# Two loads moved to ScalarE's DMA queue, and the output projection's products in another order, in a decode step of attention and feed-forward

## The chip, the cores and the metric

The kernel runs on one core of a Trainium2 chip. The metric is the device time of one execution in microseconds (us). Of the kernel before there are three timed runs: 120.58, 120.75 and 120.88, median 120.75.

The engines are TensorE (PE, with its weight loads as PEld), VectorE (DVE), ScalarE (ACT), GpSimd (POOL) and SyncE (SP). SP and ACT issue transfers between the chip's main memory and the on-chip memory, each on a queue of its own; 16 DMA engines carry them out. "SPq" and "ACTq" are the instructions of these two engines that issue. P, below, is the 128 partitions of the on-chip memory.

## The reference

For eight sequences, one token each, of width 512: a layer norm, an attention over the last 1024 positions of a cache (32 query heads, 8 cached heads, 128 wide), a GEGLU feed-forward of the same normalized token, and a product of the two:

```
xn = layernorm(x)                                  # 8 x 512
q = xn @ wq                                        # 8 x 4096: 32 heads of 128
p = softmax(q k^T / sqrt(128))                     # over 1024 positions, 4 query heads per cached head
s = (p v) @ wo                                     # 4096 x 512
g = silu((gelu(xn @ w_gate) * (xn @ w_up)) @ w_down)   # 512 -> 1792 -> 512
out = x + s * g
```

All inputs are bf16. They come to 47.5 MB: 33.6 MB of cache, wq and wo with 4.2 MB each, and the three feed-forward weights with 1.8 MB each.

## The kernel before, in words

**Order.** The kernel is written out under a manual schedule: each engine does its work in the order of the text. All loads but x are issued by SP, in this order: wo's first quarter (L106, a tile of its own, `wo_first`), wq (L109, one DMA of 4 MB), then the cache by sequence b, keys and values in two DMAs of 1 MB each (L84: k0, k1, v0, and in the loop L402 k of b+2 and v of b+1), then w_gate and w_up (L426), w_down (L429) and the rest of wo (L439). The cache tiles and the late weights go round eight slots of 2 MB (`slot`, L67); a load waits until the tile that had the slot is done with. ACT issues the five DMAs of x (L79) at the start and the store of the result (L513) at the end.

**Start.** DVE and ACT normalize x (L145 to L152), PE turns it (L166), and 32 products with wq give q (L260).

**Attention.** For each of the eight sequences DVE turns the keys into `kT` (L248), PE makes the scores (L309), DVE and ACT the softmax (L319 to L340), DVE turns the probabilities (L344), and PE multiplies them with the values (L354). `gather` (L374) and `regroup` (L376 to L398) bring the results of four sequences into `oT`, the left operand of the output projection. Its second call (L443) completes oT.

**Feed-forward.** PE makes `z_ps` and `u_ps` from w_gate and w_up (L453, 16 products each). ACT and DVE do the GELU on z: a square (L463), two DVE steps (L464, L467), a tanh (L469), and three DVE steps (L470, L471, L473) of which the last multiplies by u. DVE turns the result into `hT` (L476). PE makes `f_ps` with w_down (L482, 56 products), and ACT and DVE make the gate `g_sb` of it (L490 to L494).

**Output projection.** `wo` has four quarters u of 1024 rows. In a quarter, partition p holds rows 8p to 8p+7, as j = 0 to 7; "row j" below is that row of all 128 partitions, 128 KB. There are four products for each u and j (t = 0 to 3, a quarter of the columns each), 128 in all. They come behind w_down's products on PE, u = 0 to 3 in order, and add up in `s_ps`:

```
for u in range(NU):
    for j in range(8):
        for t in range(4):
            nc.tensor.matmul(s_ps[32 * t : 32 * t + 32, :], oT[:, j, u, :],
                wo[u][:, j, t * DT : (t + 1) * DT],
                start=(u == 0 and j == 0), stop=(u == NU - 1 and j == 7))
```

The quarter u = 3 is loaded in three pieces, rows 0 to 4, 5 and 6, and 7 (L437), so that PE can begin with the first. Then DVE multiplies `s_ps` by the gate (L509), adds x (L511), and ACT stores.

Of the kernel before, what the change touches and what calls it, by code (L numbers as in the profile page):

```python
# [11 lines left out]
FP32 = mybir.dt.float32  # L12
# [9 lines left out]
def kernel(  # L22
# [13 lines left out]
    nc = tc.nc  # L36

    B, Sq, D = A_x.shape
# [7 lines left out]
    P = nc.NUM_PARTITIONS  # L46
# [7 lines left out]
    DT = D // 4  # L54
# [12 lines left out]
    def slot(name):  # L67
        i = taken[0] % N_SLOTS
        taken[0] += 1
        if i >= 2:  # L70
            return ring.tile([P, 2 * ROW], BF16, name=name, tag="slot")
        if not late:
            late.append(ctx.enter_context(tc.tile_pool(name="late", bufs=2)))
        return late[0].tile([P, 2 * ROW], BF16, name=name, tag="slot")
# [22 lines left out]
    def load_v(b):  # L97
        v_sb[b] = load_cache(A_v_cache, b, "v_sb")

    NU = Hq // 8  # L100
    wo_src = [
        A_wo[u * 1024 : (u + 1) * 1024, :].rearrange("(p j) d -> p j d", j=8)
        for u in range(NU)
    ]
    wo_first = first.tile([P, 8, D], BF16, name="wo_first")
    nc.sync.dma_start(out=wo_first, in_=wo_src[0])  # L106
    wq_v = A_wq.rearrange("(p k) n -> p k n", k=NK)
    wq_all = wq_pool.tile([P, NK, Hq * Dh], BF16, name="wq_sb")
    nc.sync.dma_start(out=wq_all, in_=wq_v)  # L109
# [9 lines left out]
        out=ident,  # L119
        in_=ident,  # L120
# [13 lines left out]
        out=xpad,  # L134
        in_=xpad,
# [17 lines left out]
        out=xhat,  # L153
# [8 lines left out]
    with tc.tile_pool(name="ps_x", bufs=1, space=PSUM) as ps_x:  # L162
# [7 lines left out]
        for t in range(4):  # L170
# [4 lines left out]
                start=True,  # L175
                stop=True,
# [12 lines left out]
        out=hv,  # L189
        in_=hv,  # L190
# [7 lines left out]
        out=neg_st,  # L198
        in_=neg_st,
# [8 lines left out]
        out=neg_mv,  # L208
        in_=neg_mv,
# [11 lines left out]
    for g in range(NG):  # L221
        nc.vector.tensor_reduce(
            out=sel[:, g, g * qd : (g + 1) * qd],
            in_=ident.rearrange("p (t g h) -> p g h t", t=4, g=NG)[:, g],
# [5 lines left out]
        out=own, in_=ident.rearrange("p (i e) -> p e i", e=8), axis=AX.X, op=ALU.add  # L230
    )
    pick = consts.tile([P, 4 * NU], BF16, name="pick")
    with nc.allow_low_precision(reason="sums of zeros and a single one"):
        nc.vector.tensor_reduce(
            out=pick, in_=ident.rearrange("p (a e) -> p a e", e=8), axis=AX.X, op=ALU.add
        )
    oT = keep.tile([P, 8, NU, 32], BF16, name="oT")
# [18 lines left out]
    with tc.tile_pool(name="ps_q", bufs=1, space=PSUM) as ps_q:  # L256
        q_ps = [ps_q.tile([P, 512], FP32, name=f"q_ps{i}") for i in range(8)]
        for k in range(NK):
            for i in range(8):
# [4 lines left out]
                    start=(k == 0),  # L264
                    stop=(k == NK - 1),
                )
        for half in range(2):
            for i in range(4 * half, 4 * half + 4):
                e = nc.vector.tensor_copy if i % 4 == 3 else nc.scalar.copy
# [7 lines left out]
    for j in range(4):  # L277
        sl = slice(32 * j, 32 * j + 32)
        for m in range(2):
            for g in range(NG):  # L280
                e = nc.scalar.copy if (4 * j + 2 * m + g) % 3 == 2 else nc.vector.tensor_copy
# [145 lines left out]
        wgu.append(tv)  # L427
    wd = slot("wd_sb")[:, 0 : NJ * D].rearrange("p (j d) -> p j d", d=D)
    nc.sync.dma_start(out=wd, in_=B_w_down.rearrange("(p j) d -> p j d", j=NJ))  # L429
    wo = [wo_first]  # L430
    for u in range(1, NU):
        if u % 2 == 1:
            pair = slot("wo_sb").rearrange("p (v j d) -> p v j d", v=2, d=D)
        t = pair[:, (u - 1) % 2]
        pieces = [(0, 8)]
        if u == NU - 1:
            pieces = [(0, 5), (5, 7), (7, 8)]  # L437
        for a, z in pieces:
            nc.sync.dma_start(out=t[:, a:z, :], in_=wo_src[u][:, a:z, :])  # L439
        wo.append(t)  # L440

    gather(B - 1)
    regroup(1)  # L443
# [2 lines left out]
    ps_f = ctx.enter_context(tc.tile_pool(name="ps_f", bufs=1, space=PSUM))  # L446
    ffn = ctx.enter_context(tc.tile_pool(name="ffn", bufs=1))
    zu = []
    for n, ws in (("z_ps", wgu[0]), ("u_ps", wgu[1])):
        ps = ps_f.tile([P, FT], FP32, name=n)  # L450
        for k in range(NK):
            for t in range(4):
# [4 lines left out]
                    start=(k == 0),  # L457
                    stop=(k == NK - 1),
# [6 lines left out]
        out=z2, in0=z2, scalar1=0.044715, scalar2=1.0, op0=ALU.mult, op1=ALU.add  # L465
    )
    nc.vector.tensor_tensor(out=z2, in0=z2, in1=z_ps, op=ALU.mult)  # L467
    th = ffn.tile([P, FT], FP32, name="th")
    nc.scalar.activation(out=th, in_=z2, func=ACT.Tanh, scale=0.7978845608028654)  # L469
    nc.vector.tensor_scalar(out=th, in0=th, scalar1=0.5, scalar2=0.5, op0=ALU.mult, op1=ALU.add)  # L470
    nc.vector.tensor_tensor(out=th, in0=th, in1=z_ps, op=ALU.mult)  # L471
    h_bf = ffn.tile([P, FT], BF16, name="h_bf")
# [3 lines left out]
    nc.vector.transpose(  # L476
        out=hT.rearrange("p j b -> p (j b)"), in_=h_bf.rearrange("p (y j) -> p j y", j=NJ)
    )
    f_ps = ps_f.tile([P, DT], FP32, name="f_ps")
    for j in range(NJ):  # L480
        for t in range(4):
# [4 lines left out]
                start=(j == 0),  # L486
                stop=(j == NJ - 1),
# [4 lines left out]
        out=g_sb, in0=g_sb, scalar1=0.5, scalar2=0.5, op0=ALU.mult, op1=ALU.add  # L492
# [1 line left out]
    nc.vector.tensor_tensor(out=g_sb, in0=g_sb, in1=f_ps, op=ALU.mult)  # L494


    s_ps = ps_f.tile([P, DT], FP32, name="s_ps")
    for u in range(NU):
        for j in range(8):
            for t in range(4):  # L500
                nc.tensor.matmul(  # L501
                    s_ps[32 * t : 32 * t + 32, :],
                    oT[:, j, u, :],
                    wo[u][:, j, t * DT : (t + 1) * DT],
                    start=(u == 0 and j == 0),
                    stop=(u == NU - 1 and j == 7),
                )
    y = ffn.tile([P, DT], BF16, name="y")
    nc.vector.tensor_tensor(out=y, in0=s_ps, in1=g_sb, op=ALU.mult)  # L509
    out_sb = ffn.tile([P, DT], BF16, name="out_sb")  # L510
# [3 lines left out]
        out=out_f.rearrange("b (t d) -> t b d", t=4), in_=out_sb[0 : P : RB, :]  # L514
# [31 lines left out]
```

## Time and profile before

| What | before |
|---|---|
| median of three runs | 120.75 us |
| the profiled execution, its span | 120.94 us, 119.2 us |
| PE busy (products) | 68.4 us, 57% of the span |
| DVE busy | 75.8 us, 64% |
| ACT busy | 32.9 us, 28% |
| DMA | 47.57 MB, mean 399 GB/s over the span |
| SP's queue | 6048 packets, 94.6% of 16 engines' span |
| ACT's queue | 52 packets, 0.02 MB |
| instruction fetches | 7 packets, 0.10 MB |

All times are counted from the start of the span. The page of a profile cuts the span into 40 slices of 2.98 us and shows in tenths how busy each engine was, the granted clock of TensorE (PEclk), and the mean share of the 16 DMA engines. The chain of work that ended last is followed back from the last instruction, at each step to what released it. In a line of the timeline stand start, duration, engine, line of the kernel, operation, what it writes and reads, and in brackets how long the engine was idle before it, and whose end released it. Behind these views, the trace holds a record of every DMA packet (queue, start, duration, bytes) and of every signal of a landing. Those records don't name the DMA engine.

### The profile page before, as it was taken

Reading aid. Unit: us, or ns where it says so; the run is one execution under the profiler, and the core shown is the slowest. Engines: PE = TensorE matmul, PEld = TensorE weight load, DVE = VectorE, ACT = ScalarE, POOL = GpSimd, SP = SyncE. Lnnn points to the kernel's source line nnn. Section 1 sums busy time; section 2 is a strip of 40 time slices with the busy share of each in tenths; the row PEclk is TensorE's granted clock in tenths of the full one; section 3 lists DMA queues with packets and bytes.
Section 4 is the critical chain, followed back from the end, with each engine's and each line's share of the span. In section 5 each row is a group of like instructions: output and inputs, shape, how many; then the busy total and the mean of one; then the engine's idle time right before and its main releaser. Section 6 shows DMA issues by size and latency. Waiting matters only on the chain.

```text
span 119.2 us, 1740 instructions
## 1 busy us (share of the span) xinstructions
PE 68.4 (57%) x704; PEld 33.5 (28%) x704; DVE 75.8 (64%) x101; ACT 32.9 (28%) x83; POOL 3.2 (3%) x10
## 2 busy tenths in 40 slices
PE   0000189931796796969792866558359264656550
PEld 0000133410242343535340324233124132216430
DVE  1000478999999999999936995980996114273101
ACT  0300420196104336181611341071071810110000
POOL 2000070000000000000000000000000000000000
PEclk9999999999589999999999999999999955555785
DMA  3998999999999999999999999999999999999920
GB/s 102 493 463 352 393 429 423 423 432 426 421 429 423 418 437 415 418 434 429 415 429 432 418 429 429 434 421 429 423 423 429 462 409 429 443 394 434 413 104 3
DMA packets 6107, 47.57 MB, mean 399 GB/s; under 512 B 716, under 2 KB 852, under 8 KB 1108
## 3 DMA queue, kind: packets, MB, share of 16 engines
q1 hardware_dynamic: 6048, 47.45, 94.6%
q8 instruction: 5, 0.08, 0.2%
q10 hardware_dynamic: 52, 0.02, 0.1%
q14 instruction: 2, 0.02, 0.0%
HBM read 47.46 MB, written 0.01 MB: 398 GB/s over the span
## 4 chain that ended last, share of the span: by engine, by line
DMA 76%; PE 11%; DVE 6%; ACT 2%; ACTq 1%; issue 1%; DVEq 0%; SPq 0%
DMA k_sb<-in_A_k_cache_dram 32%; DMA wo_sb<-in_A_wo_dram 19%; DMA v_sb<-in_A_v_cache_dram 16%; DMA x_sb<-in_A_x_dram 9%; PE q_ps L260 8%; DVE kT L248 4%; PE S_ps L309 2%; ACTq L79 1%; ACT L161 1%; DVE mx L319 1%; PE O_ps L354 1%; DVE stats L145 1%; PE s_ps L501 1%; PE r_ps L392 1%; DVE y L509 0%
## 5 line engine op out<-in xcount | busy, mean ns | idle before, releaser
L309 PE MATMUL S_ps<-kT,qbd 128*128 128x512 bf16 x128 | 31.6, 390 | 19.4 <-DVE kT L248 16.0
L248 DVE STREAM_TRANSPOSE kT<-k_sb 128x2048 int32<-128x2048 int32 x16 | 36.6, 2290 | 5.8 <-DMA k_sb<-in_A_k_cache_dram 5.8
L309 PEld LDWEIGHTS <-qbd 128*128 128x128 bf16 x128 | 12.5, 98 | 36.6 <-issue 19.9
L329 ACT ACTIVATE nb<-m 32x1 f32<-32x1 f32 x32 | 6.4, 201 | 24.1 <-DVE m L326 23.8
L332 ACT ACTIVATE P_sb<-S_ps,nb 128x1024 bf16<-128x1024 f32 x8 | 11.1, 1387 | 0.3
L354 PE MATMUL O_ps<-v_sb,pT 128*32 128x256 bf16 x256 | 9.3, 292 | 2.7 <-DVE pT L344 2.7
L319 DVE TENSOR_REDUCE mx<-S_ps 128x1 f32<-128x1024 f32 x8 | 9.6, 1194 | 1.2 <-PE S_ps L309 1.1
L260 PE MATMUL q_ps<-wq_sb,xnR 128*128 128x512 bf16 x32 | 9.1, 457 | 0.5 <-ACT x_res L178 0.5
L366 ACT COPY O_sb<-O_ps 128x256 f32<-128x256 f32 x8 | 3.0, 373 | 21.1 <-PE O_ps L354 21.1
L166 PE MATMUL xnT_ps<-ident,xhat 8*128 8x8 bf16 x4 | 0.3, 174 | 14.6 <-DVE xhat L152 14.6
L354 PEld LDWEIGHTS <-pT 128*32 128x32 bf16 x256 | 6.5, 102 | 6.3 <-issue 3.0
L145 DVE BATCH_NORM_STATS2 stats<-x_sb 8x6 f32<-8x512 bf16 x1 | 0.7, 682 | 11.4 <-DMA x_sb<-in_A_x_dram 11.4
L344 DVE STREAM_TRANSPOSE pT<-P_sb 128x512 int32<-128x512 int32 x8 | 5.7, 711 | 3.4 <-ACT P_sb L332 2.5
L374 PE MATMUL o_ps<-O_sb,sel 128*32 128x129 f32 x32 | 5.5, 297 | 1.0 <-ACT O_sb L366 1.0
L298 PE MATMUL S_ps<-neg_mv,neg_st 128*128 128x512 bf16 x16 | 4.8, 381 | 1.9 <-DVE q_both L270 1.9
L260 PEld LDWEIGHTS <-xnR 128*128 128x128 bf16 x32 | 3.6, 114 | 5.7 <-issue 2.8
L270 ACT CAST q_both<-q_ps 128x512 bf16<-128x512 f32 x6 | 3.0, 613 | 7.8 <-PE q_ps L260 7.8
L166 PEld LDWEIGHTS <-xhat 8*128 8x128 bf16 x4 | 0.2, 114 | 14.6 <-DVE xhat L152 14.6
L374 PEld LDWEIGHTS o_ps<-O_sb,sel 128*32 128x32 f32 x32 | 3.1, 116 | 4.3 <-issue 2.5
L501 PE MATMUL s_ps<-wo_sb,oT 128*32 128x128 bf16 x96 | 2.8, 257 | 2.4 <-DMA wo_sb<-in_A_wo_dram 2.3
L251 DVE MEMSET qbd<- 128x4096 uint32 x1 | 3.5, 3472 | 0.8 <-issue 0.8
L501 PEld LDWEIGHTS <-oT 128*32 128x32 bf16 x128 | 2.9, 120 | 3.1 <-issue 2.9
(64 smaller groups left out, 48.6 us busy)
## 6 DMA issues: line engine op xcount, KB each, us to landing
k_sb<-in_A_k_cache_dram SPq DMA_DIRECT2D x16, 1024.0 KB, 19.5
v_sb<-in_A_v_cache_dram SPq DMA_DIRECT2D x16, 1024.0 KB, 19.7
wq_sb<-in_A_wq_dram SPq DMA_DIRECT2D x1, 4096.0 KB, 14.2
wo_sb<-in_A_wo_dram SPq DMA_DIRECT2D x2, 1024.0 KB
wgu_sb<-in_B_w_gate_dram SPq DMA_DIRECT2D x1, 1792.0 KB
wgu_sb<-in_B_w_up_dram SPq DMA_DIRECT2D x1, 1792.0 KB
wd_sb<-in_B_w_down_dram SPq DMA_DIRECT2D x1, 1792.0 KB, 25.1
wo_first<-in_A_wo_dram SPq DMA_DIRECT2D x1, 1024.0 KB, 4.8
```

What stands on the lines that cost most here:

```text
L248: nc.vector.transpose(out=t.bitcast(I32), in_=k_sb[b][:, g].bitcast(I32))
L251: nc.vector.memset(qbd, 0.0)
L260: nc.tensor.matmul(q_ps[i], xnR[:, k, :, :].rearrange("p j b -> p (j b)"), wq_sb[k][:, i * 512 : (i + 1) * 512], start=(k == 0), stop=(k = ...
L298: nc.tensor.matmul(S[b][:, half, :], neg_st.rearrange("p j h -> p (j h)"), neg_mv.rearrange("p a n -> p (a n)"), start=True, stop=False,)
L309: nc.tensor.matmul(S[b][:, half, :], qbd[:, m, b, w, g, :], kv[:, half * 16 : (half + 1) * 16, m, :, w], start=False, stop=(g == NG - 1 an ...
L319: nc.vector.tensor_reduce(out=mx, in_=S[b].rearrange("p a c -> p (a c)"), axis=AX.X, op=ALU.max)
L329: nc.scalar.mul(nb[32 * j : 32 * j + 32, :], m1, -inv)
L332: nc.scalar.activation(out=P_sb[b].rearrange("p c i w -> p c w i"), in_=S[b].rearrange("p a (c w i) -> p (a c) w i", w=2, i=32), func=ACT.Exp,
L344: nc.vector.transpose(out=pT[b].rearrange("p c h w -> p (c h w)").bitcast(I32), in_=P_sb[b].rearrange("p c i w -> p (c i w)").bitcast(I32),)
L354: nc.tensor.matmul(O_ps[b][32 * t : 32 * t + 32, :, :], pT[b][:, c // 2, :, c % 2], vv[:, c, :, :], start=(c < 4), stop=(c >= C - 4),)
L374: nc.tensor.matmul(o, sel[:, g, :], O_sb[b][:, g, :], start=(g == 0), stop=(g == NG - 1))
L501: nc.tensor.matmul(s_ps[32 * t : 32 * t + 32, :], oT[:, j, u, :], wo[u][:, j, t * DT : (t + 1) * DT], start=(u == 0 and j == 0), stop=(u = ...
```

## The change

wo's first quarter is issued by ACT, behind the five DMAs of x, instead of by SP ahead of wq. The last quarter gets a tile of its own, `last`, in the slot that it had before; SP loads its rows 0 to 3 and 4 in two DMAs, and ACT issues rows 5 to 7 in one, behind the tanh of the GELU. PE does the first quarter's products ahead of w_down's. Behind w_down's come the second quarter, rows 5 to 7 of the last, the third quarter, and rows 0 to 4 of the last. The count of products and DMAs stays the same. The change's label also names the store; the diff doesn't touch it.

```diff
     wo_first = first.tile([P, 8, D], BF16, name="wo_first")
-    nc.sync.dma_start(out=wo_first, in_=wo_src[0])
+    nc.scalar.dma_start(out=wo_first, in_=wo_src[0])
...
-    wo = [wo_first]
-    for u in range(1, NU):
-        if u % 2 == 1:
-            pair = slot("wo_sb").rearrange("p (v j d) -> p v j d", v=2, d=D)
-        t = pair[:, (u - 1) % 2]
-        pieces = [(0, 8)]
-        if u == NU - 1:
-            pieces = [(0, 5), (5, 7), (7, 8)]
-        for a, z in pieces:
-            nc.sync.dma_start(out=t[:, a:z, :], in_=wo_src[u][:, a:z, :])
-        wo.append(t)
+    pair = slot("wo_sb").rearrange("p (v j d) -> p v j d", v=2, d=D)
+    last = slot("wo_sb")[:, 0 : 8 * D].rearrange("p (j d) -> p j d", d=D)
+    wo = [wo_first, pair[:, 0], pair[:, 1], last]
+    for u, r, e in ((1, 0, 8), (2, 0, 8), (3, 0, 4), (3, 4, 5)):
+        nc.sync.dma_start(out=wo[u][:, r:e, :], in_=wo_src[u][:, r:e, :])
...
     nc.scalar.activation(out=th, in_=z2, func=ACT.Tanh, scale=0.7978845608028654)
+    nc.scalar.dma_start(out=last[:, 5:8, :], in_=wo_src[3][:, 5:8, :])
...
+    s_ps = ps_f.tile([P, DT], FP32, name="s_ps")
+
+    def project(rows):
+        for u, j in rows:
+            for t in range(4):
+                nc.tensor.matmul(
+                    s_ps[32 * t : 32 * t + 32, :],
+                    oT[:, j, u, :],
+                    wo[u][:, j, t * DT : (t + 1) * DT],
+                    start=(u == 0 and j == 0),
+                    stop=(u == NU - 1 and j == 4),
+                )
+
+    project((0, j) for j in range(8))
     f_ps = ps_f.tile([P, DT], FP32, name="f_ps")
...
-    s_ps = ps_f.tile([P, DT], FP32, name="s_ps")
-    for u in range(NU):
-        for j in range(8):
-            for t in range(4):
-                nc.tensor.matmul(
...
+    project((1, j) for j in range(8))
+    project((3, j) for j in (5, 6, 7))
+    project((2, j) for j in range(8))
+    project((3, j) for j in range(5))
```

More of the change, by code (lines that the diff above doesn't have):

```diff
@@ L494 @@
     nc.vector.tensor_tensor(out=g_sb, in0=g_sb, in1=f_ps, op=ALU.mult)
-    s_ps = ps_f.tile([P, DT], FP32, name="s_ps")
-    for u in range(NU):
-        for j in range(8):
-            for t in range(4):
[L501 to L507, printed above, removed]
+    project((1, j) for j in range(8))
+    project((3, j) for j in (5, 6, 7))
+    project((2, j) for j in range(8))
+    project((3, j) for j in range(5))
     y = ffn.tile([P, DT], BF16, name="y")
```

## The prediction

> **What bounds the kernel now.** I read the slices first, then the chain that ended last, then the windows at both ends of the span, and at last the trace's records of single DMA packets and landing signals.
>
> The page says that the DMA engines are full from the second slice to the last but two, at 394 to 462 GB/s from the sixth slice on, while PE is at half work:
>
> ```profile
> PE   0000189931796796969792866558359264656550
> ...
> PEclk9999999999589999999999999999999955555785
> DMA  3998999999999999999999999999999999999920
> ...
> DMA 76%; PE 11%; DVE 6%; ACT 2%; ACTq 1%; issue 1%; DVEq 0%; SPq 0%
> ```
>
> The chain in order of time has the same answer for the end. From 73.37 on it is two transfers and then the last dozen products:
>
> ```profile
> 73.37 19.65 DMA v_sb<-in_A_v_cache_dram
> 93.03 0.02 issue
> 93.04 22.27 DMA wo_sb<-in_A_wo_dram
> 115.31 0.04 issue
> 115.35 0.64 PE s_ps L501 x12
> 116.00 0.02 issue
> 116.02 0.30 DVE y L509
> 116.32 0.02 issue
> 116.35 0.22 DVE out_sb L511
> ```
>
> The 22.27 us are no slow transfer. The signals show eight semaphores in rotation: each load issues 0.01 to 0.04 us after the eighth before it has landed, so 20 us of work always stand queued. The engines never run dry: the end is set by the bytes, the first packet's time (1.82 us) and what follows the last byte (2.6 us of store and 0.6 us of DVE among it).
>
> PE in the tail, by the timeline:
>
> ```profile
> 108.42 1.68 PE L482 MATMUL f_ps<-wd_sb,hT 128*32 128x128 bf16 x56 [2.62 <-DVE hT L476]
> 109.89 1.07 PE L501 MATMUL s_ps<-wo_first,oT 128*32 128x128 bf16 x32
> 110.79 1.04 PE L501 MATMUL s_ps<-wo_sb,oT 128*32 128x128 bf16 x32
> 113.23 0.63 PE L501 MATMUL s_ps<-wo_sb,oT 128*32 128x128 bf16 x32 [1.40 <-DMA wo_sb<-in_A_wo_dram]
> 114.76 1.21 PE L501 MATMUL s_ps<-wo_sb,oT 128*32 128x128 bf16 x32 [0.90 <-DMA wo_sb<-in_A_wo_dram]
> ```
>
> PE waits for data twice after wo_first, so it has slack before the last pieces. The landing records give the rest: wo's second quarter at 110.75, third at 113.19, the pieces of the last at 114.72, 115.31 and 115.63. The last four products start at 115.68. So the last byte, not PE, starts the end.
>
> **Part 1: wo_first to ACT's queue.** SP's first load still issues at 0.81; it is wq now. ACT issues wo_first behind its five rows of x, at about 2.56 (the fifth row issues at 2.28 and takes 0.27), for some 0.37 us, the row of SP's own issue. ACT's table load behind it moves from 2.73 to about 3.1; the engine then waits until 13.61. Cost: nothing. SP is past one issue sooner, but its queue is 20 us deep: no gain.
>
> The bytes are the same on the same engines. What may differ is the first microsecond:
>
> ```profile
> 1.00:2.00 1.00, 0.00 (x0) 0.00 (x0) 0.28 (x3) 0.00 (x0) 0.57 (x3) 1.00 0.26 68
> 2.00:2.50 0.50, 0.00 (x0) 0.00 (x0) 0.00 (x0) 0.00 (x0) 0.00 (x0) 1.00 0.26 98
> 2.50:3.00 0.50, 0.00 (x0) 0.00 (x0) 0.00 (x0) 0.27 (x1) 0.00 (x0) 1.00 1.20 442
> ```
>
> The DMA share (last but one column) is only 0.26 between 2.0 and 2.5, although the first packets began at 1.82. The records show why: wo_first's 8 KB packets take 309 ns in the steady state; a first round starts at 1.82, the next bulk at 2.56, with holes between. Its eight packets per engine end between 4.50 and 5.29, where 1.85 + 8 x 0.309 is 4.32. A first packet of 32 KB (wq's, 1.22 us) would lie over such a hole. Bounds: a gain of 0.5 us, if the whole mean loss goes, and a loss of 0.1, if longer first packets spread the engines further (wq's took 1.21 to 1.44). I take a gain of 0.15, because engines that began at 2.2 or 2.6 have no hole to fill.
>
> x comes under other packets. Its last row landed at 12.57, and q's products began at 15.62, 3.05 later. The records show one engine serving x's ten packets: once wq is under way, each waits for exactly one 32 KB packet (at 8.52, 9.78, 10.99 and 12.25). Now wq is there from the start. Lower bound: strict turns from 2.4 on, the last packet at about 11.6, landing 11.9. Upper bound: all eight wq packets go first, as wo_first's eight did (1.82 + 9.8 = 11.6), then seven turns of 0.31: 13.8, landing 14.1. So q begins between 0.7 earlier and 1.5 later. That costs nothing while it stays under the 2.91 us that DVE waits for k_sb at 63.59 (a second such wait, 2.87, is at 83.15). SP's issue at 24.79, which waited for q, has some 14 us of queued loads as cover.
>
> **Part 2: the first quarter's products ahead of w_down's.** All 32 move from 109.89 into PE's idle time between u_ps (104.11 + 1.69 = 105.80) and hT (108.38): 1.07 us, over at 106.9, so w_down's products start no later. Its landing at 108.31 is the nearest thing to a limit there. What is saved at 110 goes into the wait for the second quarter: nothing on the path.
>
> **Part 3: three rows of the last quarter by ACT.** The DMA (384 KB) issues behind the tanh, at 104.97 + 0.58 = 105.6; ACT's next work is at 110.16, so nothing is queued behind it. From the rows of x: 0.94 us to the first packet (0.81 to 1.75), so 106.5; packets already taken up go first, 2.1 us (x's second packet was ready by the same 0.94 at about 2.4 and went at 4.53, behind wo_first's eight); then nine turns (eight packets of 3 KB and a signal) beside 8 KB packets. A 3 KB packet takes 122 ns between the rows of 84 (2 KB) and 196 (5 KB): 8 x (0.309 + 0.122) + 0.31 = 3.8. Signal to landing is 0.3. Landing: about 112.7. The upper bound is the 10.29 us that x's last row took: 115.9.
>
> The Trainium skill (DMA: Bandwidth & Descriptors, Queues, rings and completion order) says that an engine takes turns between queues packet by packet, a packet being some 9 to 17 descriptors. By that ACT's eight would go in a turn and land near 110; x's packets here went one for one, so the measurement decides.
>
> Until it has landed, ACT's piece holds up SP's queue by 8 x 0.122 = 0.98 us: the second quarter lands by 111.7 at the latest, the third at 114.17 (both had PE waiting), and the last pieces when they did before, since the sum of bytes is the same. Per engine the last quarter's packets come to 8 x (196 + 84 + 46) = 2608 ns before and 8 x (122 + 159 + 46) = 2616 now. The last piece is one row of 128 KB in both, so rows 0 to 3 land at about 115.3 and row 4 at 115.6.
>
> PE: third quarter 114.2 to 115.0, 16 products from 115.34, the last four by 115.66 or when the 16 are through. Here the clock counts. Products follow each other in 13 ns at granted clock 1.00 ((0.63 - 0.22) / 31) and 24 ns at 0.50 ((1.07 - 0.31) / 31). At full clock s_ps ends at 115.66 + 0.04 + 0.22 = 115.92, at half at 115.34 + 20 x 0.024 + 0.31 = 116.13; before it was 115.98. So -0.06 to +0.15; I take +0.05.
>
> The Trainium skill (TensorE: Matmul & The Clock Gate, Part 1) lets a 3.4 us window of steady work raise the clock, with the window running free. The trace agrees: 0.50 from 94.94 to 112.01, 1.00 for 3.41 us. Broken up as PE's work is after the change, it may stay at half: 116.13 rather than 115.92.
>
> **Sum.** -0.15 + 0.05 = -0.1 us. The profiled execution, 120.94 with a span of 119.2, becomes 120.85; that execution is 0.19 over the median of 120.75, so the median becomes 120.65.
>
> **Rivals.**
> *No hole at the start is filled and ACT's piece lands last (slower).* PE's order is written out: rows 5 to 7 stand ahead of the third quarter, so a late landing A holds up 12 + 32 + 20 products. It costs from A = 114.2 on. At 115.3 the end is 115.34 + 64 x 0.024 + 0.31 = 117.2, 1.2 us late: 121.9; at the bound of 115.9, 1.8: 122.5. For it: x's 10.29 us on the same queue. Against it: that was beside 32 KB packets, four times as long. 0.14.
> *The whole start-up loss goes (faster).* 0.5 gained and full clock at the tail: -0.55, 120.2; it also gains if the engines that lag change. The final signals show 11 engines through by 114.54 and five at 115.22 to 115.63, each held up by a 16 KB instruction packet (44.29, 58.68, 82.96, 99.56 and 113.09; the lag per load grows from 1.1 to 2.2 us at the first). Those packets come with PE's instructions, which stay as many. 0.27.
> *The label's store.* No line of the diff touches the store: it is ACT's before and after, worth nothing.
>
> **Numbers.** A change under 0.3% (0.36 us) can't be told from none by measurement. Forecast 0.55 (within 0.3%), faster rival 0.27, the late piece 0.14, and 0.04 for a smaller loss, say two instruction packets on one engine. So faster 0.27, same 0.55, slower 0.18. Range: from 120.0 (the faster rival and a little more) to 121.8 (a late piece, most of it).
>
> **What would show it.** Right: s_ps ends within 0.3 us of the old time after the store's issue is counted back; PE has 32 products of wo_first between u_ps and f_ps; the last DMA in the chain is SP's, and rows 5 to 7 don't wait behind the third quarter. Wrong: a PE wait for ACT's piece after 114.2; a DMA share under 0.9 in the middle of the span; DVE with no wait at 63.6 and later.

## The result, and the profile after

The changed kernel takes 121.00 us (median of 17 runs, 120.78 to 121.19) against 120.75 (17 runs, 120.58 to 120.88): ratio 1.0021, 95% interval 1.0014 to 1.0029. It is slower by 0.25 us, less than the 0.3% that the prediction took for the least difference to be told, but clear of zero, and on the other side of its forecast of -0.1. The profiled execution took 121.08 with a span of 119.4.

The page of the kernel after has the same limits, with two differences in the slices: the DMA share begins with 6 and 8 where before it began with 3 and 9, and the granted clock (PEclk) is at half for the last seven slices, without the 7, 8 of before.

```profile
PE   0000079971299497996967774797299254775550
...
PEclk9999999997559999999999999869959975555555
DMA  6899999999999999999999999999999999999920
...
DMA 75%; PE 12%; DVE 6%; ACT 2%; ACTq 1%; issue 1%; DVEq 0%; SPq 0%
```

The chain's end (start, us, what) is the old one with another number of products behind the last transfer:

```profile
93.11 22.23 DMA wo_sb<-in_A_wo_dram
115.34 0.04 issue
115.38 0.75 PE s_ps L479 x19
116.13 0.02 issue
116.15 0.30 DVE y L511
116.46 0.02 issue
116.48 0.23 DVE out_sb L513
```

The transfer in the chain, rows 0 to 3, landed at 115.34. s_ps was done 0.79 later, at 116.13, where before it was 116.00. PE's timeline of the same stretch:

```profile
105.50 1.09 PE L479 MATMUL s_ps<-wo_first,oT 128*32 128x128 bf16 x32
...
108.46 1.68 PE L491 MATMUL f_ps<-wd_sb,hT 128*32 128x128 bf16 x56 [1.87 <-DVE hT L471]
...
111.47 1.04 PE L479 MATMUL s_ps<-wo_sb,oT 128*32 128x128 bf16 x32 [1.33 <-DMA wo_sb<-in_A_wo_dram]
...
112.79 0.51 PE L479 MATMUL s_ps<-wo_sb,oT 128*32 128x128 bf16 x12 [0.28 <-DMA wo_sb<-in_A_wo_dram]
...
114.17 1.04 PE L479 MATMUL s_ps<-wo_sb,oT 128*32 128x128 bf16 x32 [0.86 <-DMA wo_sb<-in_A_wo_dram]
...
115.38 0.73 PE L479 MATMUL s_ps<-wo_sb,oT 128*32 128x128 bf16 x20 [0.17 <-DMA wo_sb<-in_A_wo_dram]
```

Read the six groups from the top: the first quarter under the GELU, w_down, the second quarter, ACT's three rows, the third quarter (1.04 us at the half clock, 0.63 before at the full one), rows 0 to 4. Each group but the first waits for something, so none is late by itself. Only the last group has more to do behind its landing: 20 products and not 12.

At the start, the windows show the hole closed, by something else than a gain. A packet's bytes and its whole duration are booked where it starts, so a share can pass 1; DMA share and GB/s are the last two columns:

```profile
1.00:2.00 1.00, 0.00 (x0) 0.00 (x0) 0.27 (x3) 0.00 (x0) 0.57 (x3) 1.00 1.42 363
2.00:2.50 0.50, 0.00 (x0) 0.00 (x0) 0.00 (x0) 0.00 (x0) 0.00 (x0) 1.00 0.74 197
2.50:3.00 0.50, 0.00 (x0) 0.00 (x0) 0.00 (x0) 0.00 (x0) 0.00 (x0) 1.00 0.32 131
```

The share is 1.42 from 1 to 2 us, where before it was 0.26: 32 KB packets lie over the time in which 8 KB packets left holes. But by the packet records, 14 of the 16 first packets took 1.8 to 2.4 us, where a later one takes 1.22. The engines are busy and little arrives.

### The profile page after: what moved, and what is told of

Read it like the earlier page. It is cut to its first block, busy times and chain, and to the rows that moved or that the text cites. A ratio compares the mean times of both kernels' runs of the same rounds, so it can differ in the third digit from the quotient of the medians.

```text
span 119.4 us, 1734 instructions
## 1 busy us (share of the span) xinstructions
PE 71.8 (60%) x697; PEld 34.8 (29%) x704; DVE 75.7 (63%) x101; ACT 32.9 (28%) x83; POOL 3.2 (3%) x10
## 4 chain that ended last, share of the span: by engine, by line
DMA 75%; PE 12%; DVE 6%; ACT 2%; ACTq 1%; issue 1%; DVEq 0%; SPq 0%
DMA k_sb<-in_A_k_cache_dram 31%; DMA wo_sb<-in_A_wo_dram 19%; DMA v_sb<-in_A_v_cache_dram 17%; DMA x_sb<-in_A_x_dram 9%; PE q_ps L260 8%; DVE kT L248 4%; PE S_ps L309 2%; ACTq L79 1%; ACT L161 1%; DVE mx L319 1%; PE O_ps L354 1%; PE s_ps L479 1%; DVE stats L145 1%; PE r_ps L392 1%; DVE y L511 0%
## 5 line engine op out<-in xcount | busy, mean ns | idle before, releaser
L309 PE MATMUL S_ps<-kT,qbd 128*128 128x512 bf16 x128 | 34.1, 413 | 16.1 <-DVE kT L248 12.4
L260 PE MATMUL q_ps<-wq_sb,xnR 128*128 128x512 bf16 x32 | 9.8, 480 | 0.5 <-ACT x_res L178 0.5
L374 PE MATMUL o_ps<-O_sb,sel 128*32 128x129 f32 x32 | 6.4, 333 | 0.9 <-ACT O_sb L366 0.9
L479 PE MATMUL s_ps<-wo_sb,oT 128*32 128x128 bf16 x96 | 3.3, 308 | 2.6 <-DMA wo_sb<-in_A_wo_dram 2.6
L479 PEld LDWEIGHTS <-oT 128*32 128x32 bf16 x128 | 3.6, 139 | 3.8 <-issue 3.6
L298 PE MATMUL S_ps<-neg_mv,neg_st 128*128 128x512 bf16 x9 | 3.3, 384 | 1.9 <-DVE q_both L270 1.9
```

Source lines behind the costliest of these rows:

```text
L260: nc.tensor.matmul(q_ps[i], xnR[:, k, :, :].rearrange("p j b -> p (j b)"), wq_sb[k][:, i * 512 : (i + 1) * 512], start=(k == 0), stop=(k = ...
L298: nc.tensor.matmul(S[b][:, half, :], neg_st.rearrange("p j h -> p (j h)"), neg_mv.rearrange("p a n -> p (a n)"), start=True, stop=False,)
L309: nc.tensor.matmul(S[b][:, half, :], qbd[:, m, b, w, g, :], kv[:, half * 16 : (half + 1) * 16, m, :, w], start=False, stop=(g == NG - 1 an ...
L374: nc.tensor.matmul(o, sel[:, g, :], O_sb[b][:, g, :], start=(g == 0), stop=(g == NG - 1))
```

## The experiments

Three theories stood against each other. **Two places**: the start loses because wq's large packets come first, and the tail loses because the half clock meets 20 products. **Queue**: taking turns with ACT's queue costs. **Late piece**: the prediction's rival, whose limit of 114.2 was not reached (ACT's rows landed at 112.75). All times are against the kernel before in the same series of runs: the ratio with its 95% interval, and the difference in us that the ratio comes to.

**Part 1 alone.** `wo_first` by ACT, all else as before:

```diff
-    nc.sync.dma_start(out=wo_first, in_=wo_src[0])
+    nc.scalar.dma_start(out=wo_first, in_=wo_src[0])
```

> Part 1 alone: ACT issues wo's first quarter, all else as before. Theory: the change lost 0.25 us in two places. About 0.1 at the start, because wq's 32 KB packets come first and the first one on each engine takes 1.8 to 2.4 us where a later one takes 1.22; about 0.15 at the end, because PE has the half clock when the last 20 products run. So this kernel should lose the start's share alone: +0.1 us (+0.05 to +0.2), with the first landing of k0 at 17.3 to 17.4 (17.24 before, 17.38 after) and the last row's landing 0.05 to 0.15 later than before's 115.63. Rival (all of the loss stems from the tail, where ACT's three rows take turns with SP's queue): 0.0.

Measured: 1.0013 (1.0002 to 1.0023), +0.16 us. Both landings came otherwise than expected: k0's first at 17.48, not at 17.3 to 17.4, and the last row at 115.42, earlier than 115.63. Single landings scatter by more than the effect, so here only the timed runs speak.

**Parts 2 and 3 alone.** The diff of the change without the line above.

> Parts 2 and 3 alone: the first quarter is SP's first load as before; the products' order and ACT's three rows are those of the change. Theory: the start is before's (k0's first landing at 17.2 to 17.3), the clock is at half in the last two us, s_ps ends 0.7 to 0.8 after rows 0 to 3 have landed; +0.15 us (+0.05 to +0.25). If the start is the whole cause: 0.0. If the turns between the queues delay the last bytes: the last landing is later than 115.7.

Measured: 1.0007 (0.9998 to 1.0016), +0.08 us. The clock was at half, and DVE's y began 0.49 behind the last landing (115.78 against 115.29), where before it was 0.39. The last landing itself was not late. The two parts add up to 1.0020, the whole is 1.0021.

**PE kept at work in the waits.**

```diff
+    warm_ps = ps_f.tile([P, 512], FP32, name="warm_ps")
+    def warm(n):
+        for _ in range(n):
+            nc.tensor.matmul(warm_ps, ident, wo_first[:, 0, :], start=True, stop=True)
...
     project((0, j) for j in range(8))
+    warm(3)
...
+    warm(3)
     project((1, j) for j in range(8))
     project((3, j) for j in (5, 6, 7))
+    warm(3)
     project((2, j) for j in range(8))
```

> The changed kernel with nine products added that nothing reads (128x128 by 128x512 into a PSUM tile of their own), three each where PE waits: behind the first quarter, behind w_down's, and behind rows 5 to 7. Theory: PE's clock is full from about 112 on, the last 20 products follow each other in 13 ns instead of 24, and s_ps ends at 115.9 to 116.0 instead of 116.13; against the change -0.1 to -0.2 us, so +0.05 to +0.15 against before. If the clock stays at half all the same, the time is the change's, +0.25, and the three products may add some of their own. Rival (the order or the queue is the cause): +0.25 with a full clock.

Measured: 1.0009 (0.9997 to 1.0021), +0.11 us, in the range. But in the profiled execution the clock was neither full nor half: 0.75 from 113.8 on. The other eleven runs had a mean granted clock of 0.89 to 0.93, those of the change 0.85 to 0.89, so the products did raise it. In that execution y began 0.43 behind the last landing, between the 0.39 of before and the 0.48 of the change. But the interval of the times just reaches the change's 1.0021, and the longer program spent 1.83 us outside the span instead of 1.73, so the time alone proves nothing.

**The three rows by SP, ahead of the third quarter**, in PE's order of the change:

```diff
-    for u, r, e in ((1, 0, 8), (2, 0, 8), (3, 0, 4), (3, 4, 5)):
+    for u, r, e in ((1, 0, 8), (3, 5, 8), (2, 0, 8), (3, 0, 4), (3, 4, 5)):
...
-    nc.scalar.dma_start(out=last[:, 5:8, :], in_=wo_src[3][:, 5:8, :])
```

> The changed kernel with rows 5 to 7 of the last quarter issued by SP between the second and the third quarter, so that PE's order is that of the change and no two queues share the engines at the end. Theory: as the change, +0.25 us (+0.15 to +0.35), since the bytes, the last piece and the clock are the same; the second quarter lands at 110.8 instead of 111.4, which PE has no use for. Rival (taking turns with ACT's queue costs): +0.1.

Measured: 1.0020 (1.0011 to 1.0028), +0.23 us (0.13 to 0.34). Without turns in the tail the loss is about the same, and the rival's +0.1 lies outside the interval; but the +0.16 of part 1 alone lies in the interval too, so the time by itself doesn't rule out a small share of the queue. Its timeline answers a second question, since here the clock happened to be full until 115.41:

```profile
114.01 0.63 PE L478 MATMUL s_ps<-wo_sb,oT 128*32 128x128 bf16 x32 [1.93 <-DMA wo_sb<-in_A_wo_dram]
115.20 0.63 PE L478 MATMUL s_ps<-wo_sb,oT 128*32 128x128 bf16 x20 [0.56 <-DMA wo_sb<-in_A_wo_dram]
```

The same 20 products take 0.63 instead of 0.73, and y begins 0.39 behind the last landing (115.88 against 115.49), as before. The full clock covered the 16 products of rows 0 to 3, which were under way before row 4 landed; row 4's four began at 115.54, 0.04 behind its landing. In the change, at half, the 16 held them up: row 4 landed at 115.67, and its products began at 115.76. The 20 products cost nothing in this execution; they cost at half.

**Part 2 alone.** The kernel before, with the first quarter's products ahead of w_down's:

```diff
+    project([0])
     f_ps = ps_f.tile([P, DT], FP32, name="f_ps")
...
+    project(u for u in range(1, NU))
```

> Part 2 alone: the kernel before with the first quarter's 32 products ahead of w_down's; loads and pieces as before. Theory: nothing on the path, 0.0 us (-0.1 to +0.1): the work goes from one wait of PE into another. What it may do is the clock: with PE idle from 110.1 to 110.8, it may stay at half to the end; then 12 products run after rows 5 and 6 have landed, 115.35 + 12 x 0.024 + 0.31 = 115.95 against a last row at 115.66 + 0.07 + 0.31 = 116.04, so s_ps ends 0.35 to 0.45 behind the last landing.

Measured: 1.0004 (0.9996 to 1.0013), +0.05 us: nothing that can be told. The clock stayed at half from 97.4 on, and y began 0.39 behind the last landing all the same. In the kernel before, too, the clock went back to half ahead of the end, at 115.42; its row for the last half microsecond has 0.50 in the column PEclk, behind POOL's:

```profile
115.50:116.00 0.50, 0.47 (x12) 0.14 (x4) 0.00 (x0) 0.00 (x0) 0.00 (x0) 0.50 0.00 0
```

So both kernels did their last four products at half, and with before's pieces (12 products) that doesn't hold up the last four: in both, these began 0.04 behind the last landing. It takes the half clock and the new pieces.

**wq ahead of wo's first quarter, both by SP.**

```diff
-    nc.sync.dma_start(out=wo_first, in_=wo_src[0])
...
     nc.sync.dma_start(out=wq_all, in_=wq_v)
+    nc.sync.dma_start(out=wo_first, in_=wo_src[0])
```

> The kernel before with wq ahead of wo's first quarter, both on SP's queue: wq's 32 KB packets come first, and no second queue takes turns. Theory (the start's share of the loss is the slow first 32 KB packet): +0.15 us (+0.05 to +0.25) as in the kernel with part 1 alone (+0.16), first packets of 1.8 to 2.4 us, k0's last landing at 17.9 to 18.0. Rival (the loss stems from ACT's queue, whose 8 KB packets and rows of x take turns with wq, or from the issue that waits for wq until 15.9): 0.0, k0's last landing at 17.75 to 17.85.

Measured: 1.0014 (1.0005 to 1.0023), +0.17 us, with no second queue beyond x's. k0's last landing came at 17.97, in the 17.9 to 18.0 expected. Its windows have nearly the start of the change:

```profile
1.00:2.00 1.00, 0.00 (x0) 0.00 (x0) 0.28 (x3) 0.00 (x0) 0.57 (x3) 1.00 1.35 363
2.00:2.50 0.50, 0.00 (x0) 0.00 (x0) 0.00 (x0) 0.00 (x0) 0.00 (x0) 1.00 0.93 262
```

The queue theory falls for the start too: it is wq in the first place that costs.

**Part 1 with wq in four DMAs.**

```diff
-    nc.sync.dma_start(out=wo_first, in_=wo_src[0])
+    nc.scalar.dma_start(out=wo_first, in_=wo_src[0])
...
-    nc.sync.dma_start(out=wq_all, in_=wq_v)
+    for k in range(NK):
+        nc.sync.dma_start(out=wq_all[:, k], in_=wq_v[:, k])
```

> Part 1 alone, with wq loaded in four DMAs of 1 MB, packets of 8 KB in place of 32 KB. Theory (size of the first packets): the start's loss goes, 0.0 us against before (-0.1 to +0.1), with a first round of 8 KB packets of 0.3 to 0.8 us and a hole behind it as before. x's turns then cost 0.31 us each and not 1.22, so x lands at 5 to 9 us in place of 12.6 to 13.2 and q's products wait for wq alone; that moves nothing at the end. Rival (ACT's queue is the cause): +0.15.

Measured: 1.0046 (1.0034 to 1.0058), +0.55 us, a miss, and not for a reason of the start. x landed in time (DVE's first statistics at 7.63 instead of 13.37). The store landed at 118.14, earlier than the 118.38 of before, but the span ended 1.14 behind it, not 0.82. The records of SP show why. With three more DMAs the store's signal fell on the semaphore that SP waits for first at the end, and five more waits stood behind it, one every 0.06 to 0.07 us: 0.31 us. The time outside the span was 1.86, against 1.73 before: 0.13 more. Without both, +0.11 us is left, with the interval's half-width of 0.14: it says nothing on the size of the packets.

**The three rows behind the gate's tanh.** ACT's DMA moved from the GELU's tanh to the gate's:

```diff
-    nc.scalar.dma_start(out=last[:, 5:8, :], in_=wo_src[3][:, 5:8, :])
...
     nc.scalar.activation(out=g_sb, in_=f_ps, func=ACT.Tanh, scale=0.5)
+    nc.scalar.dma_start(out=last[:, 5:8, :], in_=wo_src[3][:, 5:8, :])
```

> The changed kernel with ACT's DMA of rows 5 to 7 behind the gate's tanh (about 110.2) instead of the GELU's (105.1). It tests the price and the limit of the late piece: first packet at about 111.2, up to 2 us of packets ahead, nine turns of 0.43, so landing at 115 to 116.5, behind the 114.2 from which it decides. PE then has 12 + 32 + 20 products to do after it: s_ps ends at landing + 64 x 0.024 + 0.31 = 1.9 us behind it, and the kernel is 0.8 to 2 us slower than the changed one. Rival (PE overtakes, or the products are through much sooner): +0.3 or less.

Measured: 1.0144 (1.0130 to 1.0157), 122.42 us, +1.74 us, so 1.5 more than the change costs. The rows landed at 115.57, and the timeline shows the price whole:

```profile
110.56 1.05 PE L478 MATMUL s_ps<-wo_sb,oT 128*32 128x128 bf16 x32 [0.56 <-DMA wo_sb<-in_A_wo_dram]
115.61 1.90 PE L478 MATMUL s_ps<-wo_sb,oT 128*32 128x128 bf16 x64 [4.01 <-DMA wo_sb<-in_A_wo_dram]
```

PE stands 4.01 us before the missing rows, although the third quarter had landed at 113.02 and rows 0 to 3 at 114.45, then does all 64 products in 1.90.

**wq's first quarter first.** Part 1, with wq's first quarter as a DMA of its own, and x's last two rows in one:

```diff
-    for r, z in ((0, 2), (2, 4), (4, 6), (6, 7), (7, 8)):
+    for r, z in ((0, 2), (2, 4), (4, 6), (6, 8)):
...
-    nc.sync.dma_start(out=wo_first, in_=wo_src[0])
+    nc.scalar.dma_start(out=wo_first, in_=wo_src[0])
...
-    nc.sync.dma_start(out=wq_all, in_=wq_v)
+    nc.sync.dma_start(out=wq_all[:, 0], in_=wq_v[:, 0])
+    nc.sync.dma_start(out=wq_all[:, 1:], in_=wq_v[:, 1:])
```

> Part 1 with wq's first quarter as a DMA of its own (8 KB packets, one 32 KB row apart from partition to partition), the rest of wq behind it in 24 KB packets; x in four DMAs, so that the number of DMAs, and with it the order of the final waits, is before's. Theory (the size of the first packets costs the start): 0.0 us against before. Rival one (any load but wo's contiguous first quarter starts slower, by where its rows lie): +0.15. Rival two (taking turns with ACT's queue): +0.15.

Measured: 0.9990 (0.9981 to 0.9999), 120.67 against 120.78, -0.12 us. The start's loss is gone, with ACT's queue as in the change, so neither rival's +0.15 came. It is the only version here faster than the kernel before, and by so little that the interval just leaves out 1.

**k0 first.** Part 1, with SP's order k0's first half, wq, k0's second half:

```diff
-    nc.sync.dma_start(out=wo_first, in_=wo_src[0])
...
+    nc.scalar.dma_start(out=wo_first, in_=wo_src[0])
...
+    half_k0(0)
     nc.sync.dma_start(out=wq_all, in_=wq_v)
...
-    load_k(0)
+    half_k0(1)
```

> Part 1 with the first half of k0 (8 KB packets, contiguous rows) as SP's first load and wq second; wo's first quarter by ACT. Theory (size): 0.0 us against before. Rival one (where the rows lie): 0.0 too. Rival two (ACT's queue): +0.15. Together with the run that loads wq's first quarter first it tells the three apart.

Measured: 1.0019 (1.0010 to 1.0028), +0.23 us, a miss. Its first bulk packet began at 2.20 instead of 1.80: the cache's DMA takes 0.61 us to issue, and wo's 0.37:

```profile
0.80 0.61 SPq L113 DMA_DIRECT2D k_sb<-in_A_k_cache_dram  x1
1.47 0.57 SPq L121 DMA_DIRECT2D wq_sb<-in_A_wq_dram  x1
```

So this run differs in a second thing, and doesn't tell the theories apart.

**The change again**, in the same series:

> The changed kernel unaltered, on the same chip as the two others: +0.25 us (+0.15 to +0.35) against before. The clock at the tail is at half or full by the phase of its windows; s_ps ends 0.45 behind the last landing at half, 0.35 to 0.4 at full.

Measured: 1.0019 (1.0010 to 1.0029), +0.23 us; the clock was at half again, and y began 0.49 behind the last landing.

**Part 3 alone**: the change, with the first quarter's load and products as before:

```diff
-    nc.scalar.dma_start(out=wo_first, in_=wo_src[0])
+    nc.sync.dma_start(out=wo_first, in_=wo_src[0])
...
-    project((0, j) for j in range(8))
...
+    project((0, j) for j in range(8))
     project((1, j) for j in range(8))
     project((3, j) for j in (5, 6, 7))
```

> Part 3 alone: the last quarter's rows 5 to 7 by ACT and the new order behind w_down's, but the first quarter loaded by SP and its products behind w_down's as before. PE then works from 108.4 to some 110.9 and from 111.4 on, nearly as in the kernel before, so the clock should be full from about 112 to 115.4. Theory (the tail's loss is the half clock on 20 products): s_ps ends 0.35 to 0.40 behind the last landing, and the kernel is within 0.1 us of before. Rival (the 20 products behind rows 0 to 3 cost as such): 0.45 or more behind it with the full clock. If the clock is at half all the same: 0.45 to 0.48, and the first quarter's place isn't what decides over the clock.

Measured: 1.0006 (0.9997 to 1.0015), +0.07 us. The clock was full from 111.9, as expected, but its window closed at 115.36, as the last group began:

```profile
113.93 0.63 PE L479 MATMUL s_ps<-wo_sb,oT 128*32 128x128 bf16 x32 [1.49 <-DMA wo_sb<-in_A_wo_dram]
115.29 0.70 PE L479 MATMUL s_ps<-wo_sb,oT 128*32 128x128 bf16 x20 [0.73 <-DMA wo_sb<-in_A_wo_dram]
```

The third quarter ran at full speed, the last 20 products slid to half, and s_ps ended 0.56 behind the last landing, not 0.35 to 0.40. Part of that is the landing's own doing: row 4 came 0.18 behind rows 0 to 3 here, and 0.33 behind them in the change, so the 16 products had less time to get out of its way. The end of the clock's window decides over the last 20 products. That the first quarter's place moves the window is not shown: with the rows by SP the first quarter stood in its new place, and the clock was full from 111.99 to 115.41 all the same.

## Why the prediction was wrong, step by step

**The bound** was right: the end follows the last landings, and no run showed a cost in the middle of the span.

**The first microsecond** is the step that failed: "A first packet of 32 KB (wq's, 1.22 us) would lie over such a hole", a gain of 0.15. It priced the packet at its time in the middle of a stream. The first packet does lie over the hole, but takes 0.6 to 1.2 us more than a later one, which gives the hole back. Part 1 costs 0.16 us (0.02 to 0.28), wq first on SP alone 0.17 (0.06 to 0.28): a loss where the step had a gain, and with middle values beyond the loss of 0.1 that it set as its bound. What is shown: wq as one DMA in the first place costs, on either queue, and a first quarter of wq in its place doesn't.

The step's own reason for a loss, "if longer first packets spread the engines further", fits the profiles. Each engine signals its share of a load. For the first half of k0, loaded behind wo's first quarter and wq, compare the seven kernels that begin with wq's 32 KB packets with the four that begin with wo's quarter. The first engine's signal came at 17.36 and 17.39 in the mean, the average over the engines at 17.63 and 17.61, but the last engine's at 17.94 (17.84 to 18.00) and 17.84 (17.74 to 17.92). So by then about as much had arrived, and the last engine was 0.10 behind. With wq's first quarter first it was at 17.76. This is argued from single executions whose ranges overlap. That the slow first packets are the whole mechanism isn't shown: by 5.0 us the seven had moved 0.974 to 1.001 MB and the four 0.972 to 1.083, 0.08 us apart in the means at 426 GB/s, half of the loss, and the kernel that is faster than before differs in x's DMAs and in packets of 24 KB as well.

One rival has no run of its own. With wq as SP's first load, the third key DMA waited for wq's signal, and SP stood from 2.7 to 14.6 in the change and to 13.0 with wq first on SP; in the kernel before and in the one with wq's first quarter first, that DMA went at 5.6. The step left this out. Against it: by the packet records the DMA share was 1.00 or more in every stretch of 5 us from 5 to 25 us, in all these kernels.

**x** landed at 13.24, between the 11.9 and 14.1 of the prediction; q's products began at 16.29, 0.67 later than before, and cost nothing, but it was closer than worked out: at 63.20 DVE still waited for k_sb, for 0.92 us in place of 2.91.

**The first quarter's products** cost nothing, as said: over at 106.6, w_down's at 108.46 instead of 108.42, and alone +0.05 us, within its error.

**ACT's three rows** came out as worked out: landing 112.75 (112.7 predicted), second quarter 111.43 (111.7 at the latest), third 114.12 (114.17), the last pieces 115.34 and 115.67 (115.3 and 115.6), s_ps 116.13 (116.13 at half clock). Its packets went one for one with SP's: the records don't name the engine, but starts recur 0.42 us apart (108.85, 109.28, 109.70, 110.12), about 0.309 + 0.121. The Trainium skill (DMA: Bandwidth & Descriptors, Queues, rings and completion order) gives a queue typically 9 to 17 descriptors in a turn; no run here shows that. How close the landing came is in part luck. The DMA was issued at 105.09, not at 105.6, because it didn't wait for the end of the tanh (105.01 to 105.59), and its first packet began at 108.55 (108.6 worked out), so 3.46 us later and not 3.0: two errors that cancel. In the repeat of the change the same piece was issued at 103.88 and landed at 111.95.

**The clock** was a smaller error. The step put -0.06 to +0.15 and took +0.05, the middle. Half it was, in both profiles of the change. The two runs that hold the tail's new pieces without the start cost 0.08 (-0.02 to 0.19) and 0.07 (-0.04 to 0.18), neither clear of zero; the profiles are the better witness. With the old pieces y begins 0.39 to 0.40 behind the last landing in all seven kernels that have them, and in all of these the clock was at half for the last four products. With the new pieces it begins 0.48 to 0.49 behind at half (three profiles), and 0.39 where the clock was full for 16 of the 20. No profile has the last four products at the full clock.

**Sum**: -0.15 + 0.05 was forecast; +0.16 + 0.08 = 0.24 was measured alone, 0.25 together. The first term, from -0.15 to +0.16, makes up 0.31 of the 0.35 between forecast and result.

**The rival of the late piece** didn't come in, but its price was right: with the rows at 115.57 its formula gives 115.57 + 0.04 + 64 x 0.024 + 0.31 = 117.46, and s_ps ended at 117.51.

## What to carry to other kernels

In a kernel that moves bytes without a pause, moving a load between queues gained nothing here by itself; look at which packets now come first at the start, and at how many products stand behind the last landing. A written order of products is a queue: one late operand held up all that lay ready behind it, so put a price on that before moving a load behind another engine's work. Judge a closed hole in a busy row by what arrives, not by the row. And let the signs of a right forecast include one for its largest term: here all of them came true, and none looked at the first microsecond.

## What the runs showed of the hardware that was not expected

The first packets after the start are slow: in the change's profile 14 of the 16 first ones, of 32 KB, took 1.8 to 2.4 us (1.22 later), and where the first bulk packets began at 2.20 and not at 1.80 (k0 first), the first 8 KB took 0.34 to 0.47 (0.309 later).

The order of the semaphores that SP waits for at the end was worth 0.31 us in the one run in which the last signal was the first in line (wq in four DMAs).

The granted clock showed a third value: 0.75 in the profile of the run with PE kept at work, from 113.8 us on and in other stretches. No other profile here has it.
